# Attention and two-matrix MLP on one core: values loaded at full width in four parts, queries and keys by head, score tiles head by head

## The chip, the core and the metric

The program runs on one NeuronCore of a Trainium2 chip: TensorE (PE), VectorE (DVE), ScalarE (ACT) and GpSimd (POOL) compute, SyncE (SP) issues nearly all DMA transfers from one in-order queue. The time is that of the device for one execution, in microseconds.

## What is computed

Attention with a bias from relative positions (8 batch entries, 8 heads, 576 positions, 64 channels), then a gated product and two more matrix products over 4608 tokens:

```
scores = scale * q @ k.T                       # (8, 8, 576, 576)
bias   = relu((psi_rel / psi_i)[..., None] @ w1 + b1) @ w2
attn   = softmax(scores + bias)                # over keys
x      = (attn @ v) -> (4608, 512)
out    = ((x @ moe_w1) * (x @ moe_w2)) @ moe_w3 @ moe_w_out
```

## The kernel before, in words

A prologue computes the bias of all heads and writes it to DRAM (tensor `nb_d`). The attention stage then goes through 32 units, each of two heads and one batch entry (`units`, four pairs of heads by eight batch entries). At the end, the product of the last two weights is folded, and a dense stage runs to the end.

A unit's scores are cut into nine tiles of 128 query rows. Digits name them: even ones are of the first head, odd ones of the second, and tile M holds the last 64 rows of both heads. For each tile there is a step S (scores on PE, `op_S`, L251, into one of two PSUM buffers), a step T (bias added and row extreme taken on DVE, `op_T`, L262), and E (exponential on ACT with the row sum beside it, L291). Per pair of tiles there is R (32x32 block transpose on DVE into the buffer `pt`, L301; double tiles of 1152 columns, or 576 for M). When all five R of a unit are done, its products with the values start: W0 to W7 on PE (`op_W`, L338), eight parts over 18 blocks of 32 keys, one unit later than its scores. X (ACT, L347) takes the result out of PSUM and it goes to DRAM as `x_d`. Values sit in all four quarters of 32 partitions alike, so that four products of 32 rows run beside each other.

Every third unit, `r` inverts the row sums of three units on DVE (L308 to L311), and 36 small stores (`r_d`, L322 and L324) go out on SP's queue. In units 1 to 6 of each eight, one piece of the later weights is brought in as 64-bit numbers (`wi`, L131, 512 KB) and cut down in steps c0 to c7 on ACT (L136, L139), POOL and DVE. These steps stand in ACT's order between exponentials.

The order on PE, ACT, DVE and POOL follows from a table of due times (`arrange`, L38): each step has a time relative to its unit's start, and steps are recorded in the order of these times. A unit's nine tiles are planned 1.43 us apart. SP's order comes from a scheduler that sees the same program; an issue also waits until the buffer that it fills is free, and the issues behind it wait with it.

Loads before: `lk` and `lq` bring keys and queries of both heads in one transfer each (576 KB, twice replicated over partitions, L238; two buffers, so those of a unit wait for the ninth S of the unit two before). `lv` brings the values with four transfers of 288 KB (L235), each the same 32 rows of DRAM into another quarter of the partitions, also with two buffers. At the last of the eight batch entries of a pair of heads, each bias group is loaded anew as soon as its tiles are done (`load_bias`, L224, L217).

Of the kernel before, what the change touches and what calls it, by code (L numbers as in the profile page):

```python
# [9 lines left out]
F32 = mybir.dt.float32  # L10
# [8 lines left out]
P = 128  # L19
# [9 lines left out]

L_T = 1.43  # L30
PERIOD = 9 * L_T
TILES = "02134657M"
PAIRS = ("02", "13", "46", "57", "M")
NPP, NTS = 3, 3
PARTS = ((0, 3), (3, 5), (5, 7), (7, 9), (9, 12), (12, 14), (14, 16), (16, 18))


def arrange(NU, pieces):  # L38

    at = {}  # L40
    t_of = {}
    for k, t in enumerate(TILES):
        t_of[k] = (k - k % 2) * L_T + 2.0 + 0.66 * (k % 2)
        at["T" + t] = t_of[k], "DVE"
        at["E" + t] = t_of[k] + 0.75, "ACT"
    s_of = {}
    for k, t in enumerate(TILES):
        s_of[k] = t_of[k - 2] + 0.7 if k > 1 else t_of[7 + k] - PERIOD + 0.7
        at["S" + t] = s_of[k], "PE"
    for n, ts in enumerate(PAIRS[:-1]):  # L50
        at["R" + ts] = (t_of[2 * n + 2] + (1.33 if n < 3 else 0.67)), "DVE"
    at["RM"] = PERIOD + t_of[0] + 1.33, "DVE"
    at["r"] = PERIOD + t_of[0] + 1.30, "DVE"
    at["rd"] = PERIOD + t_of[0] + 2.5, "SP"
    for n in range(len(PARTS)):
        u, k = divmod(n + 3, 9)
        at[f"W{n}"] = (u + 1) * PERIOD + s_of[k] + 0.3, "PE"
    at["X"] = at["W7"][0] + 0.9, "ACT"
    at["xd"] = at["X"][0] + 0.8, "SP"
    at["lk"] = -13.0, "SP"  # L60
    at["lq"] = -12.9, "SP"
    at["lv"] = 1.2 * L_T, "SP"
    at["c0"] = 0.2, "SP"
    at["c1"] = t_of[1] + 1.6, "ACT"
    at["c2"] = t_of[3] + 1.6, "ACT"
    at["c3"] = t_of[2] + 1.0, "POOL"
    at["c4"] = t_of[4] + 1.34, "DVE"
    at["c5"] = t_of[6] + 1.34, "DVE"
    at["c6"] = t_of[8] + 0.68, "DVE"
    at["c7"] = t_of[8] + 2.0, "POOL"  # L70
    return {(n, u): (u * PERIOD + t + 1.4, e) for u in range(NU) for n, (t, e) in at.items() if n[0] != "c" or u in pieces}
# [3 lines left out]
def relpos_attention_moe(  # L75
# [17 lines left out]
    nc = tc.nc  # L93
    NPAIR, B, _, S2 = q.shape
    S, D, H = S2 // 2, P // 2, 2 * NPAIR
# [5 lines left out]
    HS = S // 2  # L101
# [93 lines left out]
    raw = att_r.enter_context(tc.tile_pool(name="raw", bufs=2, side="right"))  # L195
    nbp = att_r.enter_context(tc.tile_pool(name="nbp", bufs=1, side="right"))
    vp = att.enter_context(tc.tile_pool(name="vp", bufs=2))
# [4 lines left out]
    st = {u: {} for u in range(NU)}  # L202
# [25 lines left out]
    NBK = S // 32  # L228

    def op_l(u, which):  # L230
        p, b = units[u]
        if which == "v":
            t = vp.tile([P, 2 * NBK * D], F32, name="v4")
            for a in range(4):
                nc.sync.dma_start(t[32 * a:32 * a + 32], v[p, b])  # L235
        else:
            t = raw.tile([P, 2 * S], F32, name=which)
            nc.sync.dma_start(t, {"q": q, "k": k}[which][p, b])  # L238
        st[u][which] = t

    def op_S(u, t):

        d = st[u]
        s = d["s", t] = ps_s.tile([P, 2, 512], F32, name="s")
        for hf, rows in enumerate((lo, hi)):
            for g, outs in enumerate((lo, hi)):
                if t == "M":
                    h, q0 = g, 512
                else:
                    h, q0 = int(t) % 2, int(t) // 2 * P + 64 * g  # L250
                nc.tensor.matmul(  # L251
                    s[outs, hf, :HS], d["q"][rows, h * S + q0:h * S + q0 + 64],
                    d["k"][rows, h * S + hf * HS:h * S + (hf + 1) * HS], start=True, stop=True,
                )

    def op_T(u, t):
# [16 lines left out]
    for i in range(2):  # L273
        t = att.enter_context(tc.tile_pool(name=f"sums{i}", bufs=1)).tile([P, 32], F32, name=f"sums{i}")
        nc.gpsimd.memset(t, 1.0)
        SUMS.append(t)

    PAIR = {t: ts for ts in PAIRS for t in ts}

# [15 lines left out]

    SLOT = {t: 4 if t == "M" else int(t) // 2 + 5 * (int(t) % 2) for t in TILES}

# [28 lines left out]
    def op_W(u, n):  # L326

        d = st[u]
        if n == "0":
            d["acc"] = ps_t.tile([P, 4, 512], F32, name="acc")  # L330
        acc, pt_, x = d["acc"], PT[u % 2], d["v"]
        for b in range(*PARTS[int(n)]):
            for a in range(4):
                rows = slice(32 * a, 32 * a + 32)
                for h, outs in enumerate((lo, hi)):
                    t0, t1 = ((0, 5 if a < 2 else 4), (5 if a < 2 else 4, 9))[h]
                    c0 = 0 if (h == 1 and a >= 2) else 32
                    nc.tensor.matmul(  # L338
                        acc[outs, a, c0:c0 + 32 * (t1 - t0)], x[rows, (h * NBK + b) * D:(h * NBK + b + 1) * D],
                        pt_[rows, t0:t1, 32 * b:32 * b + 32], start=(b == 0), stop=(b == NBK - 1),  # L340
                    )

# [28 lines left out]
    def op_c(u, n):  # L371
        pieces[u][int(n)]()

    made = dict(l=op_l, S=op_S, T=op_T, E=op_E, R=op_R, r=op_r, W=op_W, X=op_X, x=op_x, c=op_c)
    later = []
    for (n, u), (at, on) in arrange(NU, pieces).items():
        step = lambda n=n, u=u: made[n[0]](u, n[1:])
        later.append((at, len(later), step, n, u))
# [8 lines left out]
    with ExitStack() as pro:  # L387
# [29 lines left out]
        def reach(G):  # L417

            return (G + 1) * GR - 1, S - 1 - G * GR
# [9 lines left out]
        for G in range(NGRP):  # L429
            n = max(reach(G)) + 1  # L430
# [42 lines left out]
        for G in range(NGRP):  # L473
            at = -LEAD + G * PACE_B
# [15 lines left out]
    PT = [pt.tile([P, 9, S], F32, name=f"pt{i}") for i in range(2)]  # L490
# [149 lines left out]
    for i in range(2 * NF):  # L640
        at = t_s + AT_F + min(i, N_F) * PACE_F0 + max(i - N_F, 0) * PACE_F
# [11 lines left out]
    for n in range(4, 2 * NF):  # L653
        at = t_s + AT_W1 + PACE_W * n
# [10 lines left out]
    for n in range(NCH * NF):  # L665
        c, ft = divmod(n, NF)
        at = t_f + STEP * n
# [62 lines left out]
```

## Time and profile before

| what | before |
|---|---|
| median of 3 runs | 1276.58 us (1274.09 to 1278.25) |
| the profiled execution | 1275.14 us |
| its span | 1273.4 us |
| PE busy | 1149.2 us (90%) |
| DVE busy | 695.9 us (55%) |
| ACT busy | 485.7 us (38%) |
| mean granted PE clock | 0.942 |
| bytes moved by DMA | 158.49 MB, mean 124 GB/s |

The span is the time from the first to the last instruction of the program; shares of busy time are means over stages with different limits, so the stages have to be read apart. A wait is listed with the engine that stood, its line, and what ended the wait. "issue" is a wait that nothing in the program's own dependences explains.

### The profile page before, as it was taken

Reading aid. Unit: us, or ns where it says so; the run is one execution under the profiler, and the core shown is the slowest. Engines: PE = TensorE matmul, PEld = TensorE weight load, DVE = VectorE, ACT = ScalarE, POOL = GpSimd, SP = SyncE. Lnnn points to the kernel's source line nnn. Section 1 sums busy time; section 2 is a strip of 40 time slices with the busy share of each in tenths; the row PEclk is TensorE's granted clock in tenths of the full one; section 3 lists DMA queues with packets and bytes.
Section 4 is the critical chain, followed back from the end, with each engine's and each line's share of the span. In section 5 each row is a group of like instructions: output and inputs, shape, how many; then the busy total and the mean of one; then the engine's idle time right before and its main releaser. Section 6 shows DMA issues by size and latency. Waiting matters only on the chain.

```text
span 1273.4 us, 34086 instructions
## 1 busy us (share of the span) xinstructions
PE 1149.2 (90%) x14720; PEld 789.4 (62%) x14720; DVE 695.9 (55%) x1293; ACT 485.7 (38%) x1071; POOL 181.1 (14%) x152
## 2 busy tenths in 40 slices
PE   7688888887788878887899999999999999999998
PEld 3234444444344434444678888888888888888887
DVE  8588786787587867879488722222213131313111
ACT  6655554464465645556445321212121112121111
POOL 0012220232022201222244500000000000000000
PEclk9978898887798888889799999999999999999999
DMA  8855769647676496675343311111202020100000
GB/s 250 283 166 166 203 176 280 189 130 228 196 223 190 120 315 177 165 206 148 118 141 109 99 50 50 50 51 36 65 33 66 33 66 34 59 36 6 8 26 33
DMA packets 61494, 158.49 MB, mean 124 GB/s; under 512 B 10400, under 2 KB 18720, under 8 KB 57248
## 3 DMA queue, kind: packets, MB, share of 16 engines
q1 hardware_dynamic: 60912, 156.30, 41.0%
q8 instruction: 115, 1.88, 0.6%
q14 instruction: 35, 0.29, 0.1%
q10 hardware_dynamic: 432, 0.02, 0.0%
HBM read 126.36 MB, written 29.92 MB: 123 GB/s over the span
## 4 chain that ended last, share of the span: by engine, by line
PE 68%; DMA 12%; DVE 7%; issue 5%; SPq 3%; ACT 3%; POOL 0%; DVEq 0%; ACTq 0%; POOLq 0%
PE up L600 31%; PE o L625 15%; PE acc L338 10%; PE s L251 9%; DMA wi<-in_moe_w_dram 3%; PE wacc L559 3%; DVE ts L262 2%; DVE pt L301 2%; DMA q<-in_q_dram 2%; DMA x_d<-x 2%; DMA nb_d<-bev 2%; SPq L322 2%; DMA nb<-nb_d 1%; ACT pp L291 1%; DMA wi<-in_moe_w_out_dram 1%
## 5 line engine op out<-in xcount | busy, mean ns | idle before, releaser
L338 PE MATMUL acc<-pt,v 32*64 32x160 f32 (+1 forms) x9216 | 260.0, 319 | 48.3 <-issue 37.3
L338 PEld LDWEIGHTS acc<-pt,v 32*64 32x64 f32 x9216 | 170.8, 143 | 180.9 <-issue 153.0
L251 PE MATMUL s<-k,q 64*64 64x288 f32 x2304 | 228.2, 471 | 53.5 <-DVE mx L262 24.2
L262 DVE CUSTOM_DVE_ANT_0 ts<-s,nb 128x576 f32<-128x576 f32 x256 | 186.9, 746 | 110.3 <-PE s L251 68.5
L608 DVE TENSOR_TENSOR g<-up,a 128x512 f32<-128x512 f32 x72 | 49.8, 692 | 342.1 <-PE up L600 342.1
L291 ACT ACTIVATE pp<-ts,mx 128x576 f32<-128x576 f32 x256 | 196.4, 769 | 82.4 <-DVE mx L262 80.5
L600 PE MATMUL up<-xh,wl 128*128 128x512 f32 x576 | 225.1, 391 | 0.0
L600 PE MATMUL up<-xl,wh 128*128 128x512 f32 x576 | 225.1, 391 | 0.0
L600 PE MATMUL up<-xh,wh 128*128 128x512 f32 x576 | 225.1, 391 | 0.0
L625 PE MATMUL o<-w3s,gh 128*128 128x512 f32 x576 | 177.7, 390 | 0.0
L301 DVE STREAM_TRANSPOSE pt<-pp 128x1152 f32<-128x1152 f32 x128 | 175.9, 1374 | 0.0
L251 PEld LDWEIGHTS s<-k,q 64*64 64x64 f32 x2304 | 68.8, 144 | 137.5 <-issue 56.0
L605 ACT COPY a<-up 128x512 f32<-128x512 f32 x72 | 42.3, 587 | 257.7 <-PE up L600 257.7
L600 PEld LDWEIGHTS up<-xl,wh 128*128 128x128 f32 x576 | 108.2, 188 | 23.4
L600 PEld LDWEIGHTS up<-xh,wl 128*128 128x128 f32 x576 | 108.2, 188 | 23.4
L600 PEld LDWEIGHTS up<-xh,wh 128*128 128x128 f32 x576 | 108.2, 188 | 23.3
L625 PEld LDWEIGHTS o<-w3s,gh 128*128 128x128 f32 x576 | 108.1, 188 | 22.9
L611 ACT ACTIVATE gh<-g 128x512 fp32r<-128x512 f32 x72 | 45.5, 632 | 178.2 <-DVE g L608 178.2
L625 PE MATMUL o<-w3s,gl 128*128 128x512 f32 x288 | 112.1, 389 | 0.0
L586 POOL TENSOR_SCALAR xh<-xr 128x512 fp32r<-128x512 f32 x36 | 23.3, 648 | 443.0 <-DVE xr L582 440.4
L142 POOL TENSOR_SCALAR wmag<-wmag 128x512 f32<-128x512 f32 x24 | 46.0, 1917 | 272.0 <-ACT wmag L136 264.3
L614 DVE TENSOR_TENSOR gl<-g,gh 128x512 fp32r<-128x512 f32 x72 | 51.9, 720 | 50.5 <-ACT gh L611 50.5
(67 smaller groups left out, 943.6 us busy)
## 6 DMA issues: line engine op xcount, KB each, us to landing
v<-in_v_dram SPq DMA_DIRECT2D x128, 288.0 KB
k<-in_k_dram SPq DMA_DIRECT2D x32, 576.0 KB
q<-in_q_dram SPq DMA_DIRECT2D x32, 576.0 KB
wi<-in_moe_w_dram SPq DMA_DIRECT2D x32, 512.0 KB
nb_d<-bev SPq DMA_DIRECT2D x36, 295.5 KB
nb<-nb_d SPq DMA_DIRECT2D x16, 576.0 KB
x_d<-x SPq DMA_DIRECT2D x32, 288.0 KB
xr<-x_d SPq DMA_DIRECT2D x36, 256.0 KB
```

What stands on the lines that cost most here:

```text
L142: clamps.tensor_scalar(d["mag"], d["mag"], LEAST, MOST, op0=ALU.max, op1=ALU.min)
L251: nc.tensor.matmul(s[outs, hf, :HS], d["q"][rows, h * S + q0:h * S + q0 + 64], d["k"][rows, h * S + hf * HS:h * S + (hf + 1) * HS], start= ...
L262: nc.vector.tensor_tensor_reduce(out=halves(ts), in0=d.pop(("s", t))[:, :, :HS], in1=halves(NB[p, t]), op0=ALU.add, op1=ALU.min, scale=-1. ...
L291: nc.scalar.activation(d["p", ps][:, k * S:(k + 1) * S], ts, AF.Exp, bias=mx, scale=-1.0, accum_out=SUMS[u // 3 % 2][:, col:col + 1],)
L301: nc.vector.transpose(o, st[u].pop(("p", ts)))
L338: nc.tensor.matmul(acc[outs, a, c0:c0 + 32 * (t1 - t0)], x[rows, (h * NBK + b) * D:(h * NBK + b + 1) * D], pt_[rows, t0:t1, 32 * b:32 * b ...
L600: nc.tensor.matmul(acc, l[:, cc], r, start=(n == 0), stop=(n == 3 * NC - 1))
L605: nc.scalar.copy(a, ps[0])
L608: nc.vector.tensor_tensor(g, ps[1], a, op=ALU.mult)
L611: nc.scalar.activation(gh, g, AF.Copy)
L614: nc.vector.tensor_tensor(gl, g, f(gh), op=ALU.subtract)
L625: nc.tensor.matmul(d["o", t], l[:, sl], folded[ft][:, r], start=(ft == 0 and n == 0), stop=(ft == NF - 1 and n == 2),)
```

## The change

Three things are changed together. The host lays the values out for all four quarters of the partitions (each row is there four times in DRAM, and the two heads lie next to each other within a block of 32 keys), and four transfers load 5, 4, 5 and 4 of the 18 blocks into 128 partitions each. Each part has its own two buffers and is due when W1, W3, W5 or W7 of the unit two before is done. Queries and keys are loaded by head, in two transfers of 288 KB each, due after the fifth and the ninth S of the unit two before. For that, the tiles go head by head: 0, 2, 4, 6, then M, then 1, 3, 5, 7. The due times of R and of the c steps on DVE are worked out for the new order. Bytes, products and their shapes stay.

```diff
-TILES = "02134657M"
-PAIRS = ("02", "13", "46", "57", "M")
+TILES = "0246M1357"
+PAIRS = ("02", "46", "M", "13", "57")
+VB = ((0, 5), (5, 9), (9, 14), (14, 18))
...
-    at["lk"] = -13.0, "SP"
-    at["lq"] = -12.9, "SP"
-    at["lv"] = 1.2 * L_T, "SP"
+    for h in range(2):
+        for k, n in enumerate("kq"):
+            at[f"l{n}{h}"] = -2 * PERIOD + s_of[4 + 4 * h] + 0.8 + 0.1 * k, "SP"
+    for c in range(4):
+        at[f"lv{c}"] = -2 * PERIOD + at[f"W{2 * c + 1}"][0] + 0.6, "SP"
...
-        if which == "v":
-            t = vp.tile([P, 2 * NBK * D], F32, name="v4")
-            for a in range(4):
-                nc.sync.dma_start(t[32 * a:32 * a + 32], v[p, b])
+        n = int(which[1])
+        if which[0] == "v":
+            b0, b1 = VB[n]
+            t = vp.tile([P, b1 - b0, 2, D], F32, name=f"v{n}")
+            src = v[p, b].rearrange("p (b h d) -> p b h d", h=2, d=D)[:, b0:b1]
+            for i in range(b0, b1):
+                st[u]["v", i] = t[:, i - b0]
         else:
-            t = raw.tile([P, 2 * S], F32, name=which)
-            nc.sync.dma_start(t, {"q": q, "k": k}[which][p, b])
-        st[u][which] = t
+            t = st[u][which] = raw.tile([P, S], F32, name=which)
+            src = {"q": q, "k": k}[which[0]][p, b][:, n * S:(n + 1) * S]
+        nc.sync.dma_start(t, src)
...
-                    s[outs, hf, :HS], d["q"][rows, h * S + q0:h * S + q0 + 64],
-                    d["k"][rows, h * S + hf * HS:h * S + (hf + 1) * HS], start=True, stop=True,
+                    s[outs, hf, :HS], d[f"q{h}"][rows, q0:q0 + 64],
+                    d[f"k{h}"][rows, hf * HS:(hf + 1) * HS], start=True, stop=True,
...
-                        acc[outs, a, c0:c0 + 32 * (t1 - t0)], x[rows, (h * NBK + b) * D:(h * NBK + b + 1) * D],
+                        acc[outs, a, c0:c0 + 32 * (t1 - t0)], d["v", b][rows, h],
...
-    a = inputs["v"].reshape(-1, pairs, 2, seq // 32, 32, dim).transpose(1, 0, 4, 2, 3, 5)
-    inputs["v"] = a.reshape(*a.shape[:3], -1)
+    a = inputs["v"].reshape(-1, pairs, 2, seq // 32, 32, dim).transpose(1, 0, 4, 3, 2, 5)
+    inputs["v"] = _np.tile(a.reshape(*a.shape[:3], -1), (1, 1, 4, 1))
```

SP's queue around the first block of row-sum stores, which goes out in unit 3. Before: `k_1723` and `q_1725` are of unit 5, `v4_1758` of unit 4, `k_1984` and `q_1986` of unit 6, `wi_1727`, `wi_1988` and `wi_2249` the weight pieces of units 4, 5 and 6.

```order
L131 DMA wi_1727<-in_moe_w_out_dram 128x1024
L322 DMA r_d0_92<-rt_1484 4x32 x2
L235 DMA v4_1457<-in_v_dram 32x2304 x4
L358 DMA x_d0_88<-x_1465 128x576
...
L238 DMA k_1723<-in_k_dram 128x1152
L238 DMA q_1725<-in_q_dram 128x1152
L235 DMA v4_1758<-in_v_dram 32x2304 x4
L358 DMA x_d0_88<-x_1766 128x576
L238 DMA k_1984<-in_k_dram 128x1152
L238 DMA q_1986<-in_q_dram 128x1152
L131 DMA wi_1988<-in_moe_w_out_dram 128x1024
L131 DMA wi_2249<-in_moe_w_out_dram 128x1024
```

The same place after the change: `k0` to `q1` with numbers 1624 to 1742 are of unit 5, `v0` to `v3` with numbers 1628 to 1800 of unit 4, `wi_2041` is the piece of unit 5.

```order
L135 DMA wi_1773<-in_moe_w_out_dram 128x1024
L329 DMA r_d0_92<-rt_1516 4x32 x2
...
L246 DMA k0_1624<-in_k_dram 128x576
L246 DMA q0_1626<-in_q_dram 128x576
L246 DMA v0_1628<-in_v_dram 128x640
L246 DMA v1_1678<-in_v_dram 128x512
L246 DMA k1_1738<-in_k_dram 128x576
L246 DMA v2_1740<-in_v_dram 128x640
L246 DMA q1_1742<-in_q_dram 128x576
L135 DMA wi_2041<-in_moe_w_out_dram 128x1024
L246 DMA v3_1800<-in_v_dram 128x512
L365 DMA x_d0_88<-x_1802 128x576
```

Between the last row-sum store and the piece of unit 5 there stood k and q of unit 5, the values of unit 4, a store, and k and q of unit 6; now k and q of unit 5 by head and three of the four parts of unit 4's values stand there, and those of unit 6 come behind.

VectorE at the start of a unit (unit 8, whose bias is `nb0_2595`, `nb1_2643` before and `nb0_2656`, `nb4_2703` after). `pt1_823` and `pt1_841` are the transposed tiles of the unit before, on which its W0 waits. Before:

```order
L262 ISA ts_2846,mx_2847<-s_2785,nb0_2595 128x576
L262 ISA mx_2847 128x1
L262 ISA ts_2853,mx_2854<-s_2818,nb0_2595 128x576
L262 ISA mx_2854 128x1
L301 STREAM_TRANSPOSE pt1_823<-ppM_2823 128x576
L262 ISA ts_2896,mx_2897<-s_2856,nb1_2643 128x576
L262 ISA mx_2897 128x1
```

And after:

```order
L269 ISA ts_2917,mx_2918<-s_2865,nb0_2656 128x576
L269 ISA mx_2918 128x1
L269 ISA ts_2921,mx_2922<-s_2889,nb0_2656 128x576
L269 ISA mx_2922 128x1
L308 STREAM_TRANSPOSE pt1_841<-pp_2870 128x1152
L269 ISA ts_2963,mx_2964<-s_2924,nb4_2703 128x576
L269 ISA mx_2964 128x1
```

The last transpose of the unit before was that of the single tile M; now it is that of the pair 5 and 7, and the reductions behind it are of the first head's tiles 4 and 6, with bias group `nb4`.

More of the change, by code (lines that the diff above doesn't have):

```diff
@@ L31 @@
 PERIOD = 9 * L_T
-TILES = "02134657M"
-PAIRS = ("02", "13", "46", "57", "M")
+TILES = "0246M1357"
+PAIRS = ("02", "46", "M", "13", "57")
 NPP, NTS = 3, 3
 PARTS = ((0, 3), (3, 5), (5, 7), (7, 9), (9, 12), (12, 14), (14, 16), (16, 18))
+VB = ((0, 5), (5, 9), (9, 14), (14, 18))
 def arrange(NU, pieces):
     at = {}
[L41 to L52, printed above, removed]
+    t_of, s_of, a = {}, {}, 2.0
+    for n, ts in enumerate(PAIRS):
+        for k, t in enumerate(ts):
+            i = len(t_of)
+            t_of[i] = a + 0.66 * k
+            at["T" + t] = t_of[i], "DVE"
+            at["E" + t] = t_of[i] + 0.75, "ACT"
+        behind = PAIRS[n - 1]
+        at["R" + behind] = a + 0.66 * len(ts) + (0.0 if n else PERIOD), "DVE"
+        a += 2 * L_T if len(ts) > 1 else L_T
+    for i, t in enumerate(TILES):
+        s_of[i] = t_of[i - 2] + 0.7 if i > 1 else t_of[7 + i] - PERIOD + 0.7
+        at["S" + t] = s_of[i], "PE"
     at["r"] = PERIOD + t_of[0] + 1.30, "DVE"
@@ L66, in arrange @@
     at["c3"] = t_of[2] + 1.0, "POOL"
-    at["c4"] = t_of[4] + 1.34, "DVE"
-    at["c5"] = t_of[6] + 1.34, "DVE"
+    at["c4"] = t_of[4] + 0.68, "DVE"
+    at["c5"] = t_of[6] + 0.68, "DVE"
     at["c6"] = t_of[8] + 0.68, "DVE"
@@ L330, in op_W @@
             d["acc"] = ps_t.tile([P, 4, 512], F32, name="acc")
-        acc, pt_, x = d["acc"], PT[u % 2], d["v"]
+        acc, pt_ = d["acc"], PT[u % 2]
         for b in range(*PARTS[int(n)]):
```

## The prediction

> **What bounds the kernel now.** I read the span first, then the three stages in the windows view (each row: window, its length, busy time of PE, PEld, DVE, ACT and POOL with instruction counts, then granted clock, DMA share, GB/s).
>
> ```profile
> span 1273.4 us, 34086 instructions
> 64.40:601.80 537.40, 445.59 (x11182) 231.64 (x11183) 426.64 (x837) 288.95 (x712) 107.16 (x72) 0.89 0.67 192
> 601.80:680.20 78.40, 68.27 (x590) 53.69 (x586) 56.90 (x84) 35.10 (x65) 30.51 (x24) 0.89 0.42 131
> 680.20:1273.40 593.20, 589.46 (x2586) 485.08 (x2584) 166.32 (x247) 119.75 (x203) 42.60 (x48) 1.00 0.14 47
> ```
>
> The profiled execution took 1275.14 us, 1.7 more than its span and 0.1% under the median of 1276.58; I sum against 1275.14. After 680 us TensorE is 99% busy at full clock and the change touches nothing there. The change acts in the attention stage, 64.4 to 601.8 us, the 32 units of two heads and one batch entry. VectorE is busy 426.6 of its 537.4 us, so 110.8 us are idle: that is all that better loads could return. Per unit that is 13.3 us busy in 16.8.
>
> Next the units one by one: a window from the first score reduction of one unit to that of the next. The first row is an undisturbed unit (number 4, from 0); the others come from a second call with the nine longest.
>
> ```profile
> 125.80:139.50 13.70, 11.24 (x332) 5.96 (x336) 13.44 (x28) 9.22 (x23) 4.52 (x4) 1.00 0.51 149
> ```
>
> ```profile
> 139.50:160.80 21.30, 18.10 (x374) 9.09 (x379) 13.73 (x27) 9.31 (x23) 4.42 (x3) 0.76 0.77 219
> ...
> 334.10:355.40 21.30, 15.27 (x396) 8.11 (x397) 12.41 (x24) 8.51 (x21) 0.00 (x0) 0.83 0.74 226
> ...
> 555.00:574.90 19.90, 18.11 (x421) 9.67 (x429) 13.58 (x26) 9.31 (x23) 3.33 (x3) 0.80 0.93 257
> sum 186.50, PE 153.45 PEld 79.97 DVE 119.11 ACT 81.23 POOL 25.88; mean PE 17.05 PEld 8.89 DVE 13.23 ACT 9.03 POOL 2.88
> ```
>
> Unit 4 runs at VectorE's pace, 13.44 of 13.70 us busy, TensorE at full clock. The nine take 186.5 us, 20.7 each, with the same VectorE work; 67.4 of the 110.8 idle us are theirs. The other 23 take 350.9 us, 15.3 each. The long ones come nearly every third unit, as the row sums do. The waits in the stage (us in total, times, longest):
>
> ```profile
> DVE ts L262 <- PE s L251: 79.2, 75, 4.7
> PE acc L338 <- issue: 34.0, 23, 4.0
> DVE ts L262 <- ACT pp L291: 17.6, 12, 4.7
> DVE ts L262 <- DMA nb<-nb_d: 17.6, 3, 11.3
> PE s L251 <- DMA q<-in_q_dram: 13.2, 4, 4.2
> ACT wmag L136 <- DMA wi<-in_moe_w_dram: 12.8, 4, 5.7
> PE s L251 <- issue: 11.5, 8, 4.0
> ACT wmag L136 <- DMA wi<-in_moe_w_out_dram: 5.3, 1, 5.3
> ```
>
> VectorE waits for scores; TensorE is late for three causes: queries not landed, ScalarE held by a weight piece that has not landed, and "issue", where nothing that the program waits for is missing. The timeline of SP's queue before unit 5 shows the first two (start, length, what is issued):
>
> ```profile
> 113.86 0.63 SPq L322 DMA_DIRECT2D r_d<-rt  x2
> 114.59 1.71 SPq L235 DMA_DIRECT2D v<-in_v_dram  x4
> ...
> 131.44 0.25 SPq L324 DMA_DIRECT2D r_d<-rt  x1
> 131.78 0.36 SPq L238 DMA_DIRECT2D k<-in_k_dram  x1
> 132.18 0.43 SPq L238 DMA_DIRECT2D q<-in_q_dram  x1
> 132.71 2.38 SPq L235 DMA_DIRECT2D v<-in_v_dram  x4
> 135.19 0.39 SPq L358 DMA_DIRECT2D x_d<-x  x1
> 135.77 0.35 SPq L238 DMA_DIRECT2D k<-in_k_dram  x1
> 136.16 0.46 SPq L238 DMA_DIRECT2D q<-in_q_dram  x1
> 138.64 3.11 SPq L131 DMA_DIRECT2D wi<-in_moe_w_out_dram  x2
> ```
>
> The 36 small stores of row sums hold the in-order queue from 113.9 to 131.7 us, 17.8 us, longer than a unit. Behind them everything starts at once: keys and queries of unit 5, values of unit 4, keys and queries of unit 6, two weight pieces. What that does to TensorE, ScalarE and VectorE:
>
> ```profile
> 138.71 0.72 PE L251 MATMUL s<-k,q 64*64 64x288 f32 x8 [2.28 <-DMA q<-in_q_dram]
> ```
>
> ```profile
> 150.90 0.66 ACT L136 ACTIVATE wmag<-wi 128x512 f32<-128x512 f32 x1 [5.29 <-DMA wi<-in_moe_w_out_dram]
> ```
>
> ```profile
> 152.35 0.76 DVE L262 CUSTOM_DVE_ANT_0 ts<-s,nb 128x576 f32<-128x576 f32 x1 [4.67 <-ACT pp L291]
> ```
>
> Scores wait 2.28 us for queries; the piece issued at 138.6 lands near 150.9; ScalarE stands at its first step from 145.6 with the exponentials behind it, and VectorE loses 4.67 us. After each gap TensorE is granted less clock (0.76 mean in unit 5, 1.00 in unit 4). Last, the rates: the first window holds keys and queries alone, the second values alone, each with the packet line of the DMA view.
>
> ```profile
> 110.00:112.00 2.00, 2.00 (x76) 1.11 (x71) 1.76 (x5) 0.00 (x0) 1.36 (x2) 1.00 0.96 364
> 116.00:119.00 3.00, 3.00 (x88) 1.43 (x80) 2.75 (x6) 2.49 (x8) 1.27 (x1) 1.00 1.05 242
> ```
>
> ```profile
> DMA packets 113, 0.73 MB, mean 242 GB/s; under 512 B 35, under 2 KB 35, under 8 KB 35
> q1 hardware_dynamic: 112, 0.71, 100.3%
> q8 instruction: 1, 0.02, 4.3%
> ```
>
> With the engines full, keys and queries into 128 partitions move 364 GB/s, values into 32 partitions 242, in packets above 8 KB. So 1.18 MB of values per unit cost 4.9 us instead of 3.2.
>
> **The change part by part.** *Earlier loads.* A part of the values or a head of keys and queries may be issued when the unit two before has used its buffer: keys and queries of the first head after the fifth tile instead of the ninth, values in four steps from W1 on instead of after W7. Each gains about half a unit of lead, some 7 us of 15.3. Waits on TensorE now stand ahead of each part in SP's queue, with weight pieces, stores and biases behind; but they follow the order in which TensorE frees buffers, and what they delay has a unit of lead, so I cost them at nothing; if that lead is gone, the price is the long units themselves.
>
> *The pile after the row sums.* By the new order seven loads stand between the last row-sum store and the piece of unit 5: 288 + 288 + 320 + 256 + 288 + 320 + 288 KB, 2.10 MB, and 0.52 MB of the piece. At 364 GB/s 2.62 MB take 7.2 us, from 131.7 to 138.9; at 242 they take 10.8, to 142.5. Either end is before 145.6, when ScalarE asks. The first head's keys and queries (0.59 MB) are in 1.6 to 2.4 us later, by 134.1, before the scores that stopped at 136.4. Their seven issues of some 0.4 us (2.8 us) lie under the transfers. So both waits of unit 5 should go. What is late next is VectorE itself: the nine units should run like the other 23, 15.3 us. That is 186.5 - 9 x 15.3 = 49; I leave half a microsecond in each, **-45**. Bounds: 0 if the 17.8 us block alone decides, -61 if they come down to 14 us.
>
> *Values at full width.* No packet above 4 KB is left among the values. The "issue" gaps hang on it:
>
> ```profile
> 294.02 1.37 PE L338 MATMUL acc<-pt,v 32*64 32x160 f32 x31 [2.50 <-issue]
> ...
> 309.24 1.24 PE L251 MATMUL s<-k,q 64*64 64x288 f32 x8 [3.96 <-issue]
> ```
>
> TensorE stops in the middle of a block of products (31 of 32 come after 2.50 us), with its instructions fetched by the same DMA engines (q8 above, one 16 KB packet among the values' packets). The gaps sum to 34.0 + 11.5 = 45.5 us. I put half of that in the nine units, where it is counted already (the 3.96 above is in one). Of the other 22 I take half, **-11**, between 0 (fetches as slow as now) and -22. [...]
>
> *Smaller transfers.* Keys and queries go in two of 288 KB in place of one of 576. The nearest row is the 364 GB/s above with several in flight; I cost it at nothing, up to the values' 242 GB/s, 1.6 us a unit, which the half unit of lead covers except in the nine: 0 to +14. [...]
>
> *The new tile order.* The last transpose of a unit, on which its products W0 wait, is now a double one; order and prices:
>
> ```profile
> L301 DVE STREAM_TRANSPOSE pt<-pp 128x1152 f32<-128x1152 f32 x128 | 175.9, 1374 | 0.0
> L301 DVE STREAM_TRANSPOSE pt<-ppM 128x576 f32<-128x576 f32 x32 | 24.3, 761 | 0.0
> ```
>
> W0 starts 1374 - 761 = 0.61 us later, 19.6 us over 32 units of TensorE time, with the scores of the fifth tile queued behind it. VectorE has two reductions and a transpose to do before it asks for that tile, and TensorE was busy 11.24 of unit 4's 13.70 us, so I take **+5**, between 0 and 19.6. The prologue carries some 0.36 MB more ahead of the biases but values load faster: within 1 us, hidden. Unit 0 now asks for the second bias group two reductions after the first; it is issued right behind the last stores, 0 to 3 us, taken as 0.
>
> Sum: 1275.1 - 45 - 11 + 5 = **1224**.
>
> **The rivals.** *Only the pile goes:* fetches stall as now, or small transfers are slow: 1275.1 - 45 + 5 = 1235. For it: the cause of "issue" is inferred from packets that run beside it. It includes values that stay at 242 GB/s from a cause other than their 32 partitions. [...]
>
> *The block decides:* the stores hold SP for 17.8 us and only half of the loss returns: -22 - 6 + 5, 1252. Against it: that block was late by only 2.28 us for the queries.
>
> *Nothing:* the loads are early, and the row-sum unit stays long by itself, 1275. Unit 4 next to unit 5 speaks against.
>
> *Slower:* TensorE becomes the bound, at W0. If it stays at reduced clock the 0.61 us add up, 19.6 us, and the loads return only the query waits of 13.2 us less 6 of other stops: 1275.1 + 19.6 - 7 = 1288. It decides from where a unit's TensorE work at the granted clock passes VectorE's 13.3 us; unit 5 with 18.10 us at 0.76 is such a unit, unit 4 is not.
>
> **How the numbers follow.** Forecast 0.62 (1224), only the pile 0.17, the block 0.10, nothing 0.04, slower 0.07. Differences under 0.3% (3.8 us) are about what a measurement of this kernel can't tell from none. Faster 0.89, same 0.04, slower 0.07. The terms' favourable ends (-61, -22, 0) give 1192, the first three cases' others 1252; leaving out about one in ten at each end, 1203 to 1257.
>
> **What would show it.** Right: the nine windows fall to 15 to 16 us, ScalarE no longer waits for weight pieces nor the scores for queries, "issue" before the products falls from 34 to under 20 us, values move near 364 GB/s, the stage takes some 486 us, and what follows 680 us keeps its 593. Wrong: long units every third, as now; values at 242; or a new wait of W0 for the transpose that reaches VectorE.

## The result, and the profile after

| what | before | after |
|---|---|---|
| median | 1275.3 us (1266.0 to 1278.3) | 1204.3 us (1203.6 to 1207.2) |
| the profiled execution | 1275.14 us | 1203.76 us |
| mean granted PE clock | 0.942 | 0.974 |
| attention stage | 537.4 us | 473.5 us |
| the nine units | 186.5 us | 155.7 us |
| the other 23 units | 350.9 us | 317.8 us |

The ratio is 0.946 [0.941, 0.951]. The forecast was 1224 with a range of 1203 to 1257: sign and range held, and the median lies 1.3 us above the favourable end. Three executions of experiment 5 ran over 1.5% longer than its fastest one and are left out there.

The page's first line and the three stages (columns as before: window, length, busy time of PE, PEld, DVE, ACT and POOL, granted clock, DMA share, GB/s):

```profile
span 1201.9 us, 34301 instructions
```

```profile
64.60:538.10 473.50, 422.50 (x11183) 219.51 (x11185) 419.09 (x837) 288.15 (x712) 107.15 (x72) 0.95 0.65 218
538.10:608.80 70.70, 64.17 (x602) 51.05 (x587) 56.49 (x83) 35.09 (x65) 30.79 (x24) 0.95 0.45 143
608.80:1201.90 593.10, 589.45 (x2585) 485.38 (x2584) 167.00 (x247) 119.60 (x203) 42.19 (x48) 1.00 0.14 47
```

The attention stage lost 63.9 us with the same 837 VectorE instructions. VectorE's idle time there fell from 110.8 to 473.5 - 419.1 = 54.4 us, which is 56.4 of the 63.9; the other 7.5 are its busy time (426.6 to 419.1), which the forecast took as fixed. TensorE is busy 23 us less with the same products: its granted clock rose from 0.89 to 0.95. What follows kept its 593 us. The short stage between shows 70.7 us for 78.4. In the kernels below it took 69 to 75 whatever was edited, so those 7.7 us can't be put down to the change; the one profile of before was the longest of all.

Unit 4, and the nine units with the same numbers as before (units 5 and 16, and the sum):

```profile
118.60:131.70 13.10, 12.57 (x365) 6.66 (x360) 13.10 (x27) 9.23 (x23) 4.48 (x3) 1.00 0.64 209
```

```profile
131.70:149.20 17.50, 13.76 (x368) 7.11 (x360) 13.63 (x28) 9.30 (x23) 4.46 (x3) 1.00 0.82 299
...
298.90:323.00 24.10, 15.49 (x368) 7.88 (x368) 12.30 (x24) 8.29 (x21) 0.00 (x0) 0.86 0.77 260
...
sum 155.70, PE 126.68 PEld 65.44 DVE 118.16 ACT 81.33 POOL 31.84; mean PE 14.08 PEld 7.27 DVE 13.13 ACT 9.04 POOL 3.54
```

Unit 4 is VectorE from end to end. The nine came down to 17.3 us each, where 15.8 was forecast, and unit 16 is longer than it was. The other 23 came down from 15.3 to 13.8, where the forecast left them nearly as they were. The waits in the stage:

```profile
DVE ts L269 <- PE s L258: 38.0, 31, 3.2
...
PE acc L345 <- issue: 16.5, 12, 2.6
...
DVE ts L269 <- DMA nb<-nb_d: 9.1, 2, 6.1
PE acc L345 <- DVE pt L308: 9.1, 20, 0.8
PE s L258 <- issue: 7.6, 6, 2.3
...
DVE ts L269 <- DMA nbM<-nb_d: 2.7, 1, 2.7
```

VectorE waits for scores 31 times in place of 75. The rows of queries not landed and of ScalarE held by a weight piece are gone, and "issue" fell from 34.0 + 11.5 to 16.5 + 7.6 = 24.1 us. SP's queue around the first block of row sums:

```profile
106.86 0.63 SPq L329 DMA_DIRECT2D r_d<-rt  x2
...
121.76 0.25 SPq L331 DMA_DIRECT2D r_d<-rt  x1
122.11 0.36 SPq L246 DMA_DIRECT2D k<-in_k_dram  x1
...
126.00 0.38 SPq L135 DMA_DIRECT2D wi<-in_moe_w_out_dram  x1
```

The block lasts 15.1 us in place of 17.8, and the piece is issued at 126.0, before unit 5 begins at 131.7; in before it came at 138.6, behind the whole pile. The rate over ten microseconds with keys, queries, values, a piece and a store in flight (no stretch of the change has the values alone for long):

```profile
132.00:142.00 10.00, 7.73 (x210) 4.10 (x213) 8.51 (x17) 5.96 (x16) 4.42 (x3) 1.00 1.03 395
```

395 GB/s, in transfers of 256 to 512 KB, where keys and queries in transfers of 576 KB moved 364 in before: with several in flight the smaller transfers show no loss of rate here.

### The profile page after: what moved, and what is told of

Its sections match the earlier page's. It is cut to its first block, busy times and chain, and to the rows that moved or that the text cites. A ratio compares the mean times of both kernels' runs of the same rounds, so it can differ in the third digit from the quotient of the medians.

```text
span 1201.9 us, 34301 instructions
## 1 busy us (share of the span) xinstructions
PE 1120.5 (93%) x14720; PEld 773.9 (64%) x14720; DVE 688.6 (57%) x1293; ACT 484.8 (40%) x1071; POOL 180.9 (15%) x152
## 3 DMA queue, kind: packets, MB, share of 16 engines
q8 instruction: 115, 1.88, 0.6%
## 4 chain that ended last, share of the span: by engine, by line
PE 67%; DVE 18%; DMA 6%; issue 6%; ACT 2%; SPq 1%; DVEq 0%; POOL 0%; ACTq 0%; POOLq 0%
PE up L607 33%; PE o L632 16%; DVE ts L269 7%; PE acc L345 7%; DVE pt L308 6%; PE s L258 6%; PE wacc L566 3%; DMA nb_d<-bev 2%; PE bacc L466 1%; DMA q<-in_q_dram 1%; DMA nb<-nb_d 1%; DVE wmag L155 1%; DMA wi<-in_moe_w_dram 1%; DMA v<-in_v_dram 1%; DMA x_d<-x 1%
## 5 line engine op out<-in xcount | busy, mean ns | idle before, releaser
L345 PE MATMUL acc<-pt,v 32*64 32x128 f32 (+1 forms) x9216 | 248.3, 301 | 27.1 <-issue 16.5
L345 PEld LDWEIGHTS acc<-pt,v 32*64 32x64 f32 x9216 | 160.3, 134 | 152.8 <-issue 109.0
L258 PE MATMUL s<-k,q 64*64 64x288 f32 x2304 | 215.5, 448 | 31.0 <-DVE mx L269 21.1
L258 PEld LDWEIGHTS s<-k,q 64*64 64x64 f32 x2304 | 65.2, 137 | 110.6 <-DVE mx L269 51.8
```

What stands on the lines that cost most here:

```text
L258: nc.tensor.matmul(s[outs, hf, :HS], d[f"q{h}"][rows, q0:q0 + 64], d[f"k{h}"][rows, hf * HS:(hf + 1) * HS], start=True, stop=True,)
L345: nc.tensor.matmul(acc[outs, a, c0:c0 + 32 * (t1 - t0)], d["v", b][rows, h], pt_[rows, t0:t1, 32 * b:32 * b + 32], start=(b == 0), stop=(b ...
```

## The experiments

Besides the medians, each kernel is read by three lengths as above: the stage, the nine units and the other 23. All compute the whole reference. Ratios are to the kernel before as it ran beside them: its median was 1270.2 us beside experiments 1 to 4 and 1269.5 and 1269.6 us beside the later ones, so the 1275.3 above is on the long side of what it does.

**1. Full width alone.** Before, with the values laid out four times; four transfers of 2304 bytes for each of 128 partitions fill the same single tile.

```diff
-                nc.sync.dma_start(t[32 * a:32 * a + 32], v[p, b])
+                nc.sync.dma_start(t[:, 576 * a:576 * a + 576], v[p, b][:, 576 * a:576 * a + 576])
...
+    inputs["v"] = _np.tile(inputs["v"], (1, 1, 4, 1))
```

> The kernel before, with the values laid out for all four quarters and loaded by four transfers of 128 partitions x 2304 bytes into the one old tile; order of tiles, of SP's queue and all due times as before. If full width is what pays (the values' 1.18 MB take 3.2 in place of 4.9 us and fetches of instructions no longer stand behind them): 1275 down to some 1240, issue gaps before products and scores from 45 us to under 25. If the earlier issue or the tile order carries the gain: 1262 or more, issue gaps may still fall.

Measured: 1222.2 us (1218.1 to 1224.2), ratio 0.963 [0.959, 0.967]. The stage took 489.8 us. The windows of the same nine units sum to:

```profile
sum 154.80, PE 133.17 PEld 69.85 DVE 117.90 ACT 81.55 POOL 31.83; mean PE 14.80 PEld 7.76 DVE 13.10 ACT 9.06 POOL 3.54
```

and the waits:

```profile
DVE ts L262 <- PE s L251: 50.6, 66, 3.4
...
PE acc L338 <- issue: 19.6, 17, 3.0
PE s L251 <- issue: 11.5, 7, 3.4
...
PE s L251 <- DMA q<-in_q_dram: 2.1, 3, 1.6
```

So all that the nine units gain in the changed kernel, 186.5 to 155, is there without an earlier load; the other 23 give 16 us more (335). One thing is not as the expectation had it: the scheduler also moved the weight pieces. SP's queue at that place:

```profile
127.47 0.37 SPq L131 DMA_DIRECT2D wi<-in_moe_w_out_dram  x1
127.94 3.86 SPq L235 DMA_DIRECT2D v<-in_v_dram  x4
```

The piece of unit 5 now stands ahead of the values, not behind all. So for the nine units width and the piece's place are not told apart by this kernel.

**2. Full width in rows of 9216 bytes.** The same with one transfer of all 128 partitions.

```diff
-            for a in range(4):
-                nc.sync.dma_start(t[32 * a:32 * a + 32], v[p, b])
+            nc.sync.dma_start(t, v[p, b])
...
+    inputs["v"] = _np.tile(inputs["v"], (1, 1, 4, 1))
```

> As the wide one, but one transfer of 128 partitions in rows of 9216 bytes: width without small packets. If the issue gaps come from large packets, they stay near 45 us and the time lies some 10 us above the wide one with small packets; if they come from the width (backlog in the queue), they fall alike and the two are within 4 us.

Measured: 1246.5 us (1238.2 to 1256.2), ratio 0.982 [0.975, 0.990]. In a profile of 1256.2 us, at the slow end of these, the stage took 517.0, the nine 161.7, the others 355.4.

```profile
PE acc L337 <- issue: 45.7, 24, 4.6
...
PE s L250 <- issue: 3.0, 5, 1.3
PE s L250 <- DMA q<-in_q_dram: 2.7, 2, 1.6
```

The queries' waits are nearly gone as in experiment 1 (2.7 and 2.1 us), and the nine fell nearly as far, but "issue" stays at 48.7 us and the other 23 gain nothing. Here the piece stands ahead of the values too.

**3. Small packets alone.** Before, with each quarter's rows cut in four pieces of 2304 bytes; still 32 partitions a transfer, and SP's queue is the old one, row for row.

```diff
-                nc.sync.dma_start(t[32 * a:32 * a + 32], v[p, b])
+                nc.sync.dma_start(
+                    t[32 * a:32 * a + 32].rearrange("p (c n) -> p c n", c=4), v[p, b].rearrange("c p n -> p c n"),
+                )
```

> The kernel before, with each quarter's rows of 9216 bytes cut into four pieces of 2304 in DRAM, still into 32 partitions: small packets without width. Large packets as the cause of issue gaps: gaps under 25 us, 1262 to 1268. Width as the cause: values stay at some 240 GB/s, gaps near 45 us, 1272 to 1278.

Measured: 1267.8 us (1265.0 to 1272.3), ratio 0.997 [0.994, 1.000]. The stage took 535.0, the nine 186.8, the others 348.2: before, to within a few microseconds.

```profile
PE acc L340 <- issue: 32.9, 20, 4.3
...
ACT wmag L136 <- DMA wi<-in_moe_w_dram: 14.2, 4, 6.0
PE s L253 <- issue: 12.5, 8, 3.6
PE s L253 <- DMA q<-in_q_dram: 8.5, 4, 2.4
```

"Issue" is 45.4 us, as in before. The rate of the values is the other half of this expectation. Here are two stretches with full engines in which nearly nothing but values moves, the first of this kernel (32 partitions, packets of 2304 bytes), the second of experiment 2 (128 partitions, 9216 bytes):

```profile
116.00:119.00 3.00, 3.00 (x101) 1.46 (x84) 2.75 (x6) 2.58 (x7) 0.75 (x1) 1.00 1.04 247
```

```profile
104.50:107.00 2.50, 2.50 (x71) 1.34 (x67) 2.36 (x6) 2.08 (x6) 0.65 (x1) 1.00 1.01 332
```

So in these stretches the rate goes with the width (242 GB/s in before, 247 here, 332 in experiment 2) and not with the packet size. The gaps don't follow the rate: neither the packet size alone (45.4) nor the width alone (48.7) shortens them; both together do (31.1). Experiment 2 also has one transfer where experiment 1 has four, and no run tells the row length from the number of transfers.

**4. Wide parts, old order and old due times.** Four wide transfers into four buffers of their own, keys and queries whole.

```diff
-            t = vp.tile([P, 2 * NBK * D], F32, name="v4")
-            for a in range(4):
-                nc.sync.dma_start(t[32 * a:32 * a + 32], v[p, b])
...
+            for n, (b0, b1) in enumerate(VB):
+                t = vp.tile([P, b1 - b0, 2, D], F32, name=f"v{n}")
...
+                nc.sync.dma_start(t, src[:, b0:b1])
```

> The kernel before with values at full width in four parts of their own buffers, so that each may be issued as the products free it; queries and keys whole, old tile order. If lead of the values matters besides width: 8 to 20 us under the wide one with one tile. If only width matters: the same within 4 us. If queries by head or the tile order carry the gain, this stays above 1235.

Measured: 1218.0 us (1210.4 to 1224.8), ratio 0.960 [0.954, 0.965]; the interval overlaps that of experiment 1, and the medians lie 4 us apart, so a gain from the buffers of their own is not shown. In its fastest execution, which is the profiled one, the stage took 479.6, the nine 150.8, the others 328.8.

```profile
DVE ts L266 <- PE s L255: 40.7, 56, 2.6
...
PE acc L342 <- issue: 23.1, 19, 2.7
...
PE s L255 <- issue: 5.0, 6, 1.6
```

"Issue" sums to 28.1 us here. By the ratios some 50 us of the 71 are here, with the old order of tiles and the old due times.

**5. The new tile order alone.** Before, with the changed kernel's tiles, pairs and due times of the tiles; loads as they were.

```diff
-TILES = "02134657M"
-PAIRS = ("02", "13", "46", "57", "M")
+TILES = "0246M1357"
+PAIRS = ("02", "46", "M", "13", "57")
```

> The kernel before with the new tile order 0246M1357 and its due times alone; loads, layout and SP's queue as before. By the forecast the order costs 0 to 20 us (the last transpose of a unit is a double one, so its products start 0.61 us later): 1275 to 1290. By the rival that the order itself pays (scores less often late for the reduction in undisturbed units): 1250 to 1268, with undisturbed units near 14 us in place of 15.3.

Measured: 1277.8 us (1264.8 to 1282.4), ratio 1.005 [1.000, 1.010]: no gain, and a loss of at most 1%. The stage took 544.3, the nine 186.6, the others 357.7. Its waits, and ahead of them the row of before that the forecast's W0 rests on:

```profile
PE acc L338 <- DVE pt L301: 3.3, 4, 1.3
```

```profile
DVE ts L263 <- PE s L252: 86.9, 61, 6.2
...
DVE ts L263 <- DMA nb<-nb_d: 17.5, 3, 8.8
...
PE acc L339 <- DVE pt L302: 8.8, 14, 1.5
```

The products' wait for the transpose grew by 5.5 us. VectorE's waits for scores grew by 7.7 and its waits for bias groups are longer too: 17.5 us where before has 6.3, each without the wait ahead of the first unit. These bias waits are a few stops where a new pair of heads begins (units 8, 16 and 24). Other kernels with the old order and late values have 9.8 to 15.3, so one profile says little on their size.

**6. The change with the old tile order.** Everything else stays; keys and queries of both heads are then free only after the ninth tile, so both are due there. The edit is that of experiment 5 backwards, and:

```diff
-            at[f"l{n}{h}"] = -2 * PERIOD + s_of[4 + 4 * h] + 0.8 + 0.1 * k, "SP"
+            at[f"l{n}{h}"] = -2 * PERIOD + s_of[8] + 0.8 + 0.1 * k, "SP"
```

> The changed kernel with the old tile order 02134657M and its due times; values wide and in parts, queries and keys by head but both free only after the ninth tile. If the order costs, this is faster than the changed kernel, below 1204; if the order pays, slower, 1215 to 1230, with undisturbed units above 14.5 us.

Measured: 1213.4 us (1206.3 to 1220.6), ratio 0.956 [0.949, 0.963], which did not part it from the change. So it was measured again beside the unchanged changed kernel:

> The changed kernel again, beside the three that follow, so that differences of under one per cent can be told: 0.946 of the kernel before, some 1203 us.

> The changed kernel with the old tile order, timed longer. Order pays with early loads (it lets the first head's keys and queries go half a unit earlier): over 0.953 of the kernel before, 1210 or more. Order neither pays nor costs: 0.943 to 0.950.

Measured: the change 1205.6 us (1202.7 to 1208.2), ratio 0.949 [0.946, 0.952]; with the old order 1217.9 (1206.8 to 1224.2), 0.958 [0.953, 0.962]. These intervals don't meet: once the loads are early, the order by head gains some 12 us, together with the half unit of lead for the first head's keys and queries that it allows; the two are not told apart. The waits with the new order, then with the old in its two profiles:

```profile
DVE ts L269 <- PE s L258: 29.0, 28, 2.9
...
PE acc L345 <- DVE pt L308: 9.5, 19, 0.8
```

```profile
DVE ts L268 <- PE s L257: 52.8, 66, 3.1
```

```profile
DVE ts L268 <- PE s L257: 42.9, 57, 2.9
```

With the old order VectorE waits 52.8 and 42.9 us for scores in 66 and 57 stops, with the new 29.0 us in 28 here and 38.0 in 31 in the profile above. The new order's W0 wait, 9.5 us on TensorE, is there, but VectorE waits less all the same. The stages took 469.3 and 487.5 us, the nine 153.3 and 163.9, the others 316.0 and 323.6. In the first pair of profiles (the change 473.5, the old order 475.4) the others fell alike, 325.4 to 317.8, but the nine did not: 150.0 with the old order, 155.7 with the new. Only the gain outside the nine, some 8 us, stands in both pairs.

**7. The change without the early values.** The four parts lie in one tile, so none may be loaded before the last product of the unit two before.

```diff
-            t = vp.tile([P, b1 - b0, 2, D], F32, name=f"v{n}")
+            if n == 0:
+                st[u]["v4"] = vp.tile([P, NBK, 2, D], F32, name="v4")
+            t = st[u]["v4"][:, b0:b1]
```

> The changed kernel with its four value parts in one tile, so that none is issued before the last product of the unit two before. If the lead of the values matters: 1212 to 1225, above all in the units after the row-sum stores; if not: 1202 to 1208.

Measured: 1215.7 us (1214.0 to 1222.1), ratio 0.959 [0.953, 0.964]; the stage took 484.9, the nine 159.6, the others 325.3.

```profile
DVE ts L271 <- PE s L260: 35.4, 41, 2.1
...
DVE ts L271 <- DMA nb<-nb_d: 19.5, 5, 7.9
```

The bias waits are at the level of experiment 5, 19.5 us where the change has 9.1 (10.1 in its second profile); on five and two stops in one profile each, that is a lead and no proof. In the time the intervals of this kernel and of the change don't meet: the early values are worth about 1%. The loss doesn't come from values that hold up the queue: SP stood 7.2 us for products in this stage, 32.9 in the change. So the two halves of the change need each other: wide parts with the old order and old due times stand at 0.960, with early values and the old order at 0.958, with the new order and late values at 0.959, with both at 0.949 (each against the kernel before beside it).

**8. The stores of the row sums, spread.** In the changed kernel unit 16 is the longest. SP's queue there:

```profile
288.49 0.78 SPq L329 DMA_DIRECT2D r_d<-rt  x2
...
303.51 0.25 SPq L331 DMA_DIRECT2D r_d<-rt  x1
303.86 0.39 SPq L228 DMA_DIRECT2D nb<-nb_d  x1
```

and VectorE's reductions:

```profile
307.88 0.76 DVE L269 CUSTOM_DVE_ANT_0 ts<-s,nb 128x576 f32<-128x576 f32 x1 [6.11 <-DMA nb<-nb_d]
...
313.28 0.76 DVE L269 CUSTOM_DVE_ANT_0 ts<-s,nbM 128x576 f32<-128x576 f32 x1 [2.67 <-DMA nbM<-nb_d]
...
320.35 0.76 DVE L269 CUSTOM_DVE_ANT_0 ts<-s,nb 128x576 f32<-128x576 f32 x1 [2.98 <-DMA nb<-nb_d]
```

The biases of the next pair of heads stand behind 15.3 us of stores, and VectorE loses 11.8 us on them. So the 36 stores were given due times of twelve in each of three units:

```diff
-    at["rd"] = PERIOD + t_of[0] + 2.5, "SP"
+    for n in range(3):
+        at[f"rd{n}"] = (1 + n) * PERIOD + t_of[0] + 2.5, "SP"
...
-        for w in range(u // 3 * 3, u + 1):
+        w = u // 3 * 3 + int(n[1])
+        if w <= u:
```

> The changed kernel with the 36 small stores of row sums spread as 12 in each of three units in place of one block. If the block of 15 us in SP's queue is what is left in the long units (17 to 18 us against 13.8): down by 15 to 25, 1180 to 1190. If the long units have another cause (biases loaded anew, the reciprocal itself): within 4 us of 1204.

> The changed kernel with the 36 row-sum stores in three lots of 12, timed longer. If one block is what is left to lose: under 0.940. If the stores cost the same wherever SP issues them: 0.943 to 0.950.

Measured: 1197.8 us (1193.6 to 1204.1), 0.944 [0.938, 0.950]; again, beside the change: 1199.5 (1196.7 to 1209.2), 0.946 [0.941, 0.950]. The interval overlaps the change's 0.949 [0.946, 0.952]. The nine units fell to 148.3 and 146.4 us and unit 16 to 20.7 and 17.1, but the others rose to 326.7 and 324.0; the stage, 475.1 and 470.4, is that of the change. That this kernel is faster than the change is not shown.

SP's queue around the first stores shows why it is no test of a spread:

```profile
106.71 0.63 SPq L331 DMA_DIRECT2D r_d<-rt  x2
...
113.84 0.36 SPq L247 DMA_DIRECT2D k<-in_k_dram  x1
...
126.97 0.24 SPq L333 DMA_DIRECT2D r_d<-rt  x1
```

All 36 go out from 106.7 to 127.2 us, in 20.5 us in place of 15.1, with loads between them. Only around unit 16 do they stretch further, from 291 to 324 us. So the run shows the stores interleaved with loads: what the nine gain by it, 7 us, the others lose. What twelve stores in each of three units would do stays open.

**9. The stores recorded behind the last unit.**

```diff
-        for w in range(u // 3 * 3, u + 1):
-            sums_out(w, st[u]["rt"][:], 9 * (w % 3))
+        if u == NU - 1:
+            for w in range(NU):
+                sums_out(w, st[min(w // 3 * 3 + 2, u)]["rt"][:], 9 * (w % 3))
```

> The changed kernel with all row-sum stores put off to the end of the attention stage; its whole time is longer by their issue, some 100 us, and only the attention stage is read. If the block of stores makes the long units that are left: the nine fall from 155 to some 130 us and the stage from 473 to 450. If biases loaded anew and fetches make them: stage over 462.

Measured, in a single execution and so without an interval: 1196.8 us; the stage took 465.7, the nine 143.7, the others 322.0, unit 16 17.3. The scheduler didn't leave the stores at the end: from 107 us on they stand among the loads again, in nearly the places of experiment 8. So the run isn't the bound on the block that it was meant to be; it repeats experiment 8 more than it adds to it.

## Why the prediction was right, and where its sum was not

**What bounds the kernel** was right: VectorE in the attention stage, its idle time as nearly the whole prize, "issue", queries and weight pieces as the causes. Most signs named came: no wait for queries or pieces, "issue" before the products 16.5 us, 395 GB/s in mixed traffic, 593 us kept behind. One did not: the nine units stand at 17.3 us, not at 15 to 16. The stage fell 63.9 us where 51 was the sum. Two terms were mis-sized in opposite directions and cancelled in part, which is luck: the nine gave 30.8 us for 45, the other 23 units 33.1 for the 6 that -11 and +5 left them. Of the 71.4 us between the two profiled executions another 7.7 lie in the short stage, which no term priced.

**The pile after the row sums, -45**, was too large: the nine units gave 31 us and stand 13.5 us above the 9 x 15.8 that the step set. Of these, 8.3 are unit 16 alone (24.1 us): its biases stand behind the block of stores, and the step has no term for them. The step also let the gaps of the nine go with the pile, but 19.5 of 24.0 us of "issue" are still there (3.0 us before the products of unit 5, whose reductions wait 3.4 us for scores). How much of the rest the block of stores keeps up is not shown, since experiments 8 and 9 did not take it apart. The reason was also narrower than stated. The step credits the loads that now stand behind the block in other places, and the queue shows them there; but experiment 1 takes the nine to 154.8 us without the earlier loads. Small packets with the old queue (experiment 3) and the new order with old loads (experiment 5) leave them at 187, so it isn't chance that the same nine are long. Whether the width or the weight piece's place ahead of the values does it stays open: in each kernel with wide values the scheduler moved the piece as well. In the nine, VectorE's waits for exponentials, behind which the pieces stand, fell from 15.8 to 1.4 us in experiment 1, and its waits for scores from 42.4 to 25.1, so what the pieces held up directly is about half of the gain.

**Values at full width, -11**, was too small, in the right direction. The other 23 units gave 16 us in experiment 1, 22 in experiment 4 and 33 in the change. The split of the gaps that the step assumed was right: of before's 45.4 us, 24.0 lie in the nine and 21.4 outside. Outside they fell to 16.2 us in experiment 1, to 13.4 in experiment 4 and to 4.5 in the change, so by 17 us at last where the step took 11. In VectorE's own time outside the nine, its waits for scores fell from 36.8 to 20.1 us, its reductions' other waits from 7.8 to nothing, and its busy time from 307.5 to 300.9; the step priced the gaps alone. That slower products behind the gaps are what it left out is not shown: the granted clock rose mostly in the nine, 0.79 to 0.93, and outside from 0.94 to 0.96.

What the step inferred, that the gaps are instruction fetches, the traces of before and of the change bear out. Queue q8 brings instructions in packets of 16 KB (115 for 1.88 MB), 86 of them in the stage of before, one in some 6 us. All 17 "issue" gaps of over 1 us in that stage, 37.6 of the 45.4 us, end 1.3 to 1.7 us after the end of such a packet; so do all 11 in the stage of the change, 19.7 of its 24.0 us. The gap that ends at 294.02 in the prediction has its packet in the window 291.0 to 292.3, of which these are the queues, and none from 292.4 to 294.0:

```profile
q1 hardware_dynamic: 47, 0.29, 93.3%
q8 instruction: 1, 0.02, 5.9%
```

What holds such a packet up beside the values is not shown; that wide and small packets together shorten the gaps is, from one profile of each kernel. Two profiles of one kernel (experiment 6, old order) gave 23.9 and 34.3 us, so the step from 45 to 31 is larger than that scatter, but not by much.

**Earlier loads, 0, and the new tile order, +5,** should have been one term. Apart neither shows a gain: order alone 1.005 [1.000, 1.010], early values with the old order no better than wide parts alone. Together they take the kernel from 0.958 to 0.949, and the 23 units from 324 to 316. The price named in the step came true, W0's wait rose from 3.3 to 9.1 us, but it was covered: VectorE's waits for scores fell. By what the pair of them gains stays open. Fewer bias waits are not it: with early loads the new order has 9.1 and 10.1 us of them, the old order 5.3 and 6.9.

**Smaller transfers, 0,** is not contradicted: 395 GB/s with several in flight. No run has the small transfers of keys and queries alone. The one large transfer of 1.18 MB in experiment 2 made the slowest of the wide kernels (1246.5 us), though with longer rows too.

**The rivals.** "Only the pile goes" (1235) is refuted by the gaps that fell outside the nine, and by the 33 us there. Its form in which the values stay at 242 GB/s is not borne out either: into 128 partitions they moved 332 in experiment 2. "The block decides" (1252) is refuted as the main case, since the nine gave 31 us with the block in place; what it still costs is open. "Nothing" is refuted by the time. "Slower" by W0 is refuted, since TensorE was busy 23 us less, at a higher granted clock.

## What to carry to other kernels

When an operand has to lie in several partition quarters, look at the width and the packet size of its load before its due time: here a copy in DRAM that fills 128 partitions in rows of some 2 KB gave 3.7% alone, and either property without the other gave about half of that or less. A gap on TensorE may cost more than its length, since its granted clock can be lower behind it (0.50 after one of 2.28 us, the row below), so value gaps by the units that have them against the units that don't. Edits to order and to lead should be costed together, because here neither showed its worth without the other. After an edit of due times, read the queue in the trace before reading the time: twice here the scheduler had put the stores elsewhere.

## What the runs showed of the hardware

- The "issue" gaps of TensorE, 45.4 us in the attention stage of before, differed with how the values were moved: 45.4 with packets of 2304 bytes into 32 partitions, 48.7 with 9216 bytes into 128, 31.1 with 2304 bytes into 128, 24.1 in the change (one profile each). Neither property alone moved them, which was not expected. All 28 of these gaps over 1 us in the attention stages of before and of the change end 1.3 to 1.7 us after the end of a 16 KB instruction packet.
- Values moved at 242 and 247 GB/s into 32 partitions, in packets of 9216 and 2304 bytes, and at 332 into 128 partitions in packets of 9216.
- At equal width and bytes, rows of 9216 bytes in one transfer lost about half of the gain of rows of 2304 in four: 0.982 [0.975, 0.990] against 0.963 [0.959, 0.967].
- Thirty-six small stores occupy SP's queue for 13 to 15 us in the change and 17 to 19 in before (some 0.3 us each, and gaps), about a unit of attention.
- After the gap of 2.28 us in unit 5 of before, which ends at 138.7, the granted clock was 0.50 (the last but two of this row) while TensorE was busy throughout. The prediction has less clock after each gap; not each one has it: after the one of 1.94 us that ends at 175.1 it stayed at 1.00.

```profile
140.00:143.00 3.00, 3.00 (x56) 1.40 (x48) 1.65 (x5) 0.00 (x0) 2.00 (x2) 0.50 0.97 294
```
